# First four-head chunk inside the loop, and early half loads of the first values, in a cached decode-attention kernel

## The chip, the cores, the metric

One core of one Trainium2 chip. The metric is the device time of one execution in microseconds (us), median of several runs. All runs here are of the state called fast; with one core there is no other die to compare with.

## The reference, cut to what matters

Two independent decode attentions, one query token for each of four batch entries, bf16. Part A has 32 query heads on 8 key/value heads and looks at the last 2048 keys only. Part B has 32 heads of its own and looks at all 8192 keys. Part B's caches make up 537 MB of the 587 MB read.

```python
def _B_ref(x, k_cache, v_cache, wq, wo):        # A: the same with k, v repeated and Sk cut to W
    B, Sq, D = x.shape                          # 4, 1, 512
    H, Dh = 32, 128
    q = (x @ wq).reshape(B, Sq, H, Dh).transpose(0, 2, 1, 3)
    scores = jnp.einsum("bhqd,bhkd->bhqk", q, k_cache) * (Dh ** -0.5)   # Sk = 8192
    p = _softmax(scores, axis=-1)
    o = jnp.einsum("bhqk,bhkd->bhqd", p, v_cache)
    return o.transpose(0, 2, 1, 3).reshape(B, Sq, H * Dh) @ wo
```

## The kernel before

The work is cut into chunks: 8 of part A, then 32 of part B (four heads of one batch entry each). A chunk of part B has 8.39 MB of keys K and 8.39 MB of values V. TensorE transposes the keys (group `tr`), multiplies them with the query (`sc`), and after the softmax multiplies the values with the probabilities (`po`). In what follows the chunks of part B are called b0, b1, b2 and so on.

Pass c of part B does the keys of chunk c and the values of the chunk before. For b0 there is no chunk before, so it runs an "empty" value pass (`NONE`): 256 matmuls with probabilities of zero over whatever the value buffer holds. This keeps all passes alike.

```python
def whole_B(c):
    ch, p = chunks[c], prev(c)          # prev(first chunk) is NONE
    sch.mark()
    emit_qb(c)
    for g in range(ch["NG"]):           # 32 groups of 8 tiles
        emit_T(ch["s"] + g)             # transposes
        ...
    exp_B(c)                            # after out_B(p): values of the chunk before
```

All loads go through one transfer queue, in program order. Each has to wait until its buffer is free. Keys come in two halves (free when a half has been transposed), values as one transfer (free when the value pass has ended):

```python
def dma_B(kind, c):
    ...
    if kind == "k":
        pieces, fam = (NTB // 2,) * 2, "d_bk"
    else:
        pieces, fam = (LASTV, "d_lv") if c == NC - 1 else (NEXTV, "d_nv") if c == NC - 2 else ((NTB,), "d_bv")
    for i, n in enumerate(pieces):
        ...
        if kind == "v" and c == NCA:
            waits += [("pv", NONE)]     # V(b0) after the empty pass
        sch.add_dma("sp", ..., waits=waits, key=(kind, c, i))
    for u in range(4):
        held[at + u] = [("T", ...) if kind == "k" else ("pv", c)]

for c in range(NCA, NC):                # order: K(b0), K(b1), V(b0), K(b2), V(b1), ...
    dma_B("k", c)
    ...
    dma_B("v", c - 1)
```

A recording layer finds equal passes and emits them as one loop per engine. The first pass may join the loop if its waits, written with the loop's counter, are no weaker than its own. On TensorE and VectorE b0 did not qualify, so it stood as straight-line code ahead of the loop. For the head of TensorE's second loop the kernel asks for `head_slot` 0, taken here as the start of a block of 256 instruction slots (an estimate from the spacing of stalls, below), and a jump over padding leads into it.

Of the kernel before, what the change touches and what calls it, by code (L numbers as in the profile page):

```python
# [13 lines left out]
TG = 8  # L14
# [5 lines left out]
NSM = 2  # L20
SLAG = 2
NW = 64
NEXTV = (128, 64, 64)
LASTV = (128, 64, 32, 16, 8, 8)
QK = (0, 16)
# [2 lines left out]
TRM0, BC0, L0, Q0, XT0 = 0, 256, 288, 320, 448  # L28
# [19 lines left out]
class _Sched:  # L48
# [88 lines left out]
    def moved(self, ops, says, w, v, n, step, less=False):  # L137
        if says[w[0]:w[1]] != says[v[0]:v[1]]:
            return False
        new = dict(step)  # L140
        for k in range(w[1] - w[0]):
            x, y = self.needs(ops[w[0] + k][1]), self.needs(ops[v[0] + k][1])
            if ops[w[0] + k][3] is not None:
                x[k], y[k] = ops[w[0] + k][3], ops[v[0] + k][3]
            if less:
                if any(c not in x or y[c] > x[c] + n * new[c] for c in y) or any(x[c] + n * new[c] <= 0 for c in x):
                    return False
            elif set(x) != set(y) or any(y[c] - x[c] != n * new.setdefault(c, (y[c] - x[c]) // n) for c in x):
                return False
        step.update(new)  # L150
        return True
# [14 lines left out]
def bass_concat_heads__sliding_block_cached__mha_block_cached__decode_kernel(  # L166
# [29 lines left out]
    NC = len(chunks)  # L196
    NCA = Hkv
# [8 lines left out]
    NTA, NTB = chunks[0]["NT"], chunks[-1]["NT"]  # L206
    NONE = NC
    chunks.append(dict(chunks[NCA]))
    assert sum(LASTV) == sum(NEXTV) == NTB and NTA * 16 == 1024 and NTB * 4 == 1024

    sch = _Sched()
    with ExitStack() as es:
        block = es.enter_context(nc.Block())

        def sb(name, shape, dt):
            return es.enter_context(nc.sbuf_tensor(name, shape, dt))

        def ps(name, shape, dt):
            return es.enter_context(nc.psum_tensor(name, shape, dt))
# [3 lines left out]
        wos = sb("wos", [P, 4, DO], BF16)  # L223
        qb = sb("qb", [P, 2, NW], BF16)
        qq = sb("qq", [P, NW], BF16)
        wor = sb("wor", [P, NWO, 4 * DO], BF16)
        xs = sb("xs", [NB, 2, D], BF16)
        xT = sb("xT", [P, 2, KC * NB], BF16)
        qs = sb("qs", [P, 2 * NB * HQ + NW], BF16)
        identb = sb("identb", [P, P], BF16)  # L230
        identf = sb("identf", [P, P], F32)
        onesf = sb("onesf", [P, P], F32)
# [13 lines left out]
        pm = sb("pm", [P, HB + 1, NB, 4], F32)  # L246
        pbt = {0: sb("pba", [P, NPB, NTA * 16 + NW], BF16), 1: sb("pbb", [P, 1, NTB * 4 + NW], BF16)}
        oT = sb("oT", [P, NSM, 16], BF16)
# [8 lines left out]
        ms = ps("ms", [P, 512], F32)  # L257
# [2 lines left out]

        semnames = ["eng_pe", "eng_dve", "eng_act", "eng_pool", "eng_sp", "d_x0", "d_x1", "d_o0", "d_o1", "r_k", "r_v"]
        semnames += ["d_h%d" % i for i in range(NH)] + ["d_bk0", "d_bk1", "d_bv0"]
        semnames += [f + str(i) for f, x in (("d_lv", LASTV), ("d_nv", NEXTV)) for i in range(len(x))]
        semnames += ["d_wo%d" % i for i in range(NWO)] + ["d_wos"]
        sems = {n: es.enter_context(nc.semaphore(n)) for n in semnames}

# [12 lines left out]
        for u in range(4):  # L279
            sch.add("pool", lambda e, u=u: e.memset(rst[1][u * P // 4:(u + 1) * P // 4, u:u + 1], 1.0),  # L280
                    waits=["c_rs0"], key="c_rs" if u == 3 else None)
# [19 lines left out]
        held = [[] for _ in range(NH)]  # L301
# [10 lines left out]
        def flat(at, n):  # L312
            return kv[:, at:at + n, :].rearrange("p s x -> p (s x)")
# [21 lines left out]
        def dma_wos(hq):  # L335


            src = B_wo[4 * hq * P:4 * (hq + 1) * P, :].rearrange("(p r) n -> p (r n)", r=4)
            sch.add_dma("sp", lambda e: e.dma_start(wos[:, :, :].rearrange("p r n -> p (r n)"), src), "d_wos",
                        waits=[("fin", NCA + 4 * hq - 1)] if hq else [], key=("wos", hq))  # L340
# [6 lines left out]
            src = T[:, ch["g"], SkA - W:, :].rearrange("b (pp j) d -> pp b (j d)", pp=P // NB)  # L347
            sch.add_dma("sp", lambda e: e.dma_start(kv[:, at, :], src), "d_h%d" % at, waits=waits, key=(kind, c))

        def dma_B(kind, c):  # L350


            ch = chunks[c]
            T, at = (B_k, KB) if kind == "k" else (B_v, VB if c < NC - 1 else KB)
            src = T[ch["b"], 4 * ch["hq"]:4 * ch["hq"] + 4].rearrange("u (pp j) d -> (u pp) (j d)", pp=P // 4)
            dst = flat(at, 4)
            if kind == "k":
                pieces, fam = (NTB // 2,) * 2, "d_bk"
            else:
                pieces, fam = (LASTV, "d_lv") if c == NC - 1 else (NEXTV, "d_nv") if c == NC - 2 else ((NTB,), "d_bv")  # L360
            j0, unit = 0, NTB // 4
            for i, n in enumerate(pieces):
                waits = []
                for u in range(j0 // unit, (j0 + n - 1) // unit + 1):
                    waits += held[at + u]
                if kind == "v" and c == NCA:
                    waits += [("pv", NONE)]
                x = slice(j0 * P, (j0 + n) * P)
                sch.add_dma("sp", lambda e, x=x: e.dma_start(dst[:, x], src[:, x]), fam + str(i), waits=waits, key=(kind, c, i))
                if kind == "k" or c < NC - 1:  # L370
                    sch.relay("pool", sems, "r_" + kind, n // TG,
                              [(kind, c, i)] + ([("wos", ch["hq"])] if kind == "v" and i == 0 and ch["b"] == 0 else []))
                j0 += n
            for u in range(4):
                held[at + u] = [("T", ch["s"] + (u + 1) * unit // TG - 1) if kind == "k" else ("pv", c)]

        def landed(kind, c, g):

# [23 lines left out]
        for c in range(NCA, NC):  # L402
            dma_B("k", c)
            if c == NCA:
                dma_wos(0)
                sch.relay("pool", sems, "r_v", NTB // TG, [("wos", 0)])
                continue
            if c > NCA + 1 and (c - 1 - NCA) % NB == 0:
                dma_wos((c - 1 - NCA) // NB)
            dma_B("v", c - 1)  # L410
        dma_B("v", NC - 1)

        ms_read = []
        po_read = []
        rs_read = [[] for _ in range(NSM + 1)]

        def pe_mm(o, l, r, start=True, stop=True, transpose=False, waits=(), key=None):
            if transpose:
                sch.add("pe", lambda e: e.transpose(o, l, r), waits, key)  # L419
            else:  # L420
                sch.add("pe", lambda e: e.matmul(o, l, r, start=start, stop=stop), waits, key)  # L421
# [81 lines left out]
        def emit_S(s):  # L503
            c, g = groups[s]
            ch = chunks[c]
            for t in range(TG):
# [5 lines left out]

                n = min(NW, 512 - o0)
                q = qb[:, c % 2, 0:n] if ch["ab"] == 0 else qq[:, 0:n]
# [28 lines left out]
        def par(c):  # L543
            return c % 2 if c < NCA else 0
# [88 lines left out]
        def emit_pv(c, g):  # L633
            ch = chunks[c]
            UC = ch["UC"]
            base = 16 * (c % NSM) if ch["ab"] == 0 else 0
            for t in range(TG):
                j = g * TG + t
                n = NW
                waits = ([("exp", c)] if c != NONE else [("c_pb", 1)]) + po_read if j == 0 else []  # L640
                if j == 0:
                    po_read[:] = []
                if c >= NCA:
                    waits += landed("v", c, g) if t == 0 else []
                elif j == 0:
                    waits += [("v", c)]
                pe_mm(po[:, base:base + n], tile_of("v", c, j), pbt[ch["ab"]][:, par(c), j * UC:j * UC + n],
                      start=j == 0, stop=j == ch["NT"] - 1, waits=waits, key=("pv", c) if j == ch["NT"] - 1 else None)

        def norm_sum(c):  # L650
            if c < NCA:
                m, n, rs, ri = c % NSM, 16, rst[0][:, c % NSM, :], rinv[:, c % NSM, :]
            else:
                m, n, rs, ri = NSM, 4, rst[1][:, :], rinv[:, 0, 0:4]
            pe_mm(ms[:, L0:L0 + n], onesf[:, :], rs, waits=[("rs", c) if c != NONE else "c_rs", "c_onesf"] + ms_read, key=("L", c))
            sch.add("dve", lambda e: e.reciprocal(out=ri, in_=ms[:, L0:L0 + n]), waits=[("L", c)], key=("rinv", c))
            if c >= NCA:

                col = 16 * (c - NCA + 1 if c != NONE else 0)
                pv = pm[:, :, :, :].rearrange("p a b u -> p (a b u)")  # L660
                sch.add("dve", lambda e, x=0: e.tensor_tensor(
                    out=rz[:, :].rearrange("p (b u) -> p b u", b=NB), in0=bcast(ri, [[0, NB], [1, 4]]),
                    in1=pv[:, bass.ds(x + col, 16)].rearrange("p (b u) -> p b u", b=NB), op=ALU.mult),
                    waits=[("rinv", c), "c_pm"], key=("rz", c), at=col)
            ms_read[:] = [("rinv", c)]
            rs_read[m] = [("L", c)]
# [221 lines left out]
```

## Time and profile before

| | before |
|---|---|
| median of the runs on record with the result | 1393.03 us (1388.76 to 1394.37, 4 runs) |
| span of the profiled run | 1390.7 us |
| TensorE busy | 85% |
| read from memory | 587.21 MB, 422 GB/s over the span |

The prediction below shows the page, the windows and the transfer queue's timeline. One more view is needed to judge it afterwards: TensorE's timeline in b1's pass, the first time round the loop. Each line is start, length, engine, source line, operation, operands and count, and in brackets the idle time ahead of it with what ended it. "issue" means that nothing the profile records was waited for.

```profile
182.76 0.40 PE L419 MATMUL tr<-identb,kv 128*128 128x128 bf16 x4 [0.83 <-issue]
...
189.21 0.62 PE L419 MATMUL tr<-identb,kv 128*128 128x128 bf16 x8 [1.06 <-issue]
...
195.37 0.68 PE L421 MATMUL sc<-qq,kt 128*128 128x64 bf16 x20 [0.66 <-issue]
```

I read these, like the 7.51 us at the jump, as TensorE waiting for code, and call them code stalls. The DMA view, asked in steps of 0.1 us, has a packet of the instruction queue that starts at 180.5, 186.9 and 193.0 us, 2.3 to 2.4 us ahead of these three lines, as it has one at 165.9 us, 2.6 us ahead of the first line after the jump. The three lines stand 124 matmuls apart, and two such stalls inside a value pass stand 128 apart (shown below). A matmul counts as two instruction slots (the page has 27295 matmuls and as many weight loads), so a block of code is taken as 256 slots, an estimate from this spacing. The packets of the instruction queue are of 16 KB each (24 packets, 0.39 MB). In later passes of the loop the stalls do not occur: between 250 and 1340 us the view of waits lists none without a releaser, and the instruction queue has no such packet.

### The profile page before, as it was taken

What the parts mean: (1) busy time and instruction counts of PE and PEld (TensorE: products, weight loads), DVE (VectorE), ACT (ScalarE), POOL (GpSimd) and SP (SyncE); (2) the same over time, 40 slices, a digit from 0 to 9 for tenths busy, and PEclk for the clock granted to TensorE, in tenths of its full rate; (3) what the DMA queues carried; (4) which work ended last, traced back from release to release, by engine and by line L of the source; (5) the groups of instructions that cost most, each with busy time, mean ns of one, the idle gap of its engine ahead of it and who ended that gap; (6) DMA issues with size and microseconds to landing.
All of it is one profiled execution on the core that took longest, in us unless ns stands there. A gap on an engine that the chain in (4) does not pass through costs nothing.

```text
span 1390.7 us, 60414 instructions
## 1 busy us (share of the span) xinstructions
PE 1177.1 (85%) x27295; PEld 1124.9 (81%) x27295; DVE 682.5 (49%) x1532; ACT 482.1 (35%) x651; POOL 6.8 (0%) x27
## 2 busy tenths in 40 slices
PE   4898688888888878888888888888988878888887
PEld 4787688888887878888888778888878878888886
DVE  1776245555444444555444445555444444555442
ACT  1553223333333333333333332333333332333331
POOL 1000000000000000000000000000000000000000
PEclk9999899999999999999999999999999999999999
DMA  9999879999999999999999999999999999999998
GB/s 398 426 427 398 361 308 407 436 430 432 449 424 424 435 430 431 437 432 430 449 424 426 435 429 431 435 434 429 448 424 426 435 431 430 435 434 433 444 415 344
DMA packets 19797, 587.66 MB, mean 423 GB/s; under 512 B 2212, under 2 KB 2232, under 8 KB 4664
## 3 DMA queue, kind: packets, MB, share of 16 engines
q1 hardware_dynamic: 19736, 587.21, 98.4%
q8 instruction: 24, 0.39, 0.1%
q14 instruction: 5, 0.04, 0.0%
q10 hardware_dynamic: 32, 0.01, 0.0%
HBM read 587.21 MB, written 0.01 MB: 422 GB/s over the span
## 4 chain that ended last, share of the span: by engine, by line
DMA 62%; PE 33%; DVE 2%; issue 2%; SPq 0%; ACT 0%; DVEq 0%; POOLq 0%
DMA kv<-in_B_v_cache_dram 58%; PE po L421 22%; PE tr L419 6%; PE sc L421 3%; DMA kv<-in_B_k_cache_dram 2%; DMA kv<-in_B_wq_dram 2%; PE ms L421 1%; PE fin L421 1%; DVE sA L539 1%; DVE zB L698 0%; DVE rh L556 0%; DVE rm L551 0%; DVE kt L486 0%; DVE sA L537 0%; PE ms L419 0%
## 5 line engine op out<-in xcount | busy, mean ns | idle before, releaser
L419 PE MATMUL tr<-identb,kv 128*128 128x128 bf16 x8704 | 658.7, 220 | 13.3 <-issue 9.8
L486 DVE COPY kt<-tr 128x1024 bf16<-128x1024 bf16 x736 | 499.2, 691 | 212.9 <-PE tr L419 211.3
L419 PEld LDWEIGHTS tr<-identb,kv 128*128 128x128 bf16 x8704 | 509.4, 99 | 23.7 <-issue 19.0
L484 ACT ACTIVATE kt<-tr 128x1024 bf16<-128x1024 bf16 x352 | 359.3, 1023 | 388.1 <-PE tr L419 377.9
L421 PE MATMUL sc<-qq,kt 128*128 128x64 bf16 x8192 | 398.1, 191 | 11.1 <-DVE kt L486 9.5
L421 PE MATMUL po<-pbb,kv 128*128 128x64 bf16 x8448 | 312.0, 207 | 57.2 <-POOLq L70 55.0
L421 PEld LDWEIGHTS po<-pbb,kv 128*128 128x128 bf16 x8448 | 307.5, 108 | 60.3 <-POOLq L70 57.2
L421 PEld LDWEIGHTS sc<-qq,kt 128*128 128x128 bf16 x8192 | 328.7, 98 | 21.6 <-DVE kt L486 12.9
L596 ACT ACTIVATE pbb<-sc,negb 32x256 bf16<-32x256 f32 x128 | 105.4, 823 | 498.0 <-PE po L421 496.5
L678 DVE TENSOR_TENSOR oz<-po,rz 128x16 bf16<-128x16 f32 x33 | 5.8, 175 | 363.4 <-PE po L421 363.4
L556 DVE TENSOR_REDUCE rh<-sc 32x1 f32<-32x128 f32 x256 | 73.1, 286 | 17.2 <-PE sc L421 14.7
L419 PE MATMUL ms<-identf,rm 128*1 128x128 f32 (+1 forms) x40 | 11.4, 285 | 50.5 <-DVE rm L559 47.2
L419 PEld LDWEIGHTS ms<-identf,rm 128*1 128x1 f32 (+1 forms) x40 | 3.2, 80 | 54.4 <-DVE rm L559 50.1
L421 PE MATMUL fin<-wos,zB 128*4 128x256 bf16 x264 | 19.9, 272 | 26.6 <-DVE zB L698 26.1
L421 PEld LDWEIGHTS ms<-identf,gx 1*128 1x128 f32 (+1 forms) x80 | 13.5, 211 | 28.0 <-DVE gx L575 26.5
L421 PE MATMUL ms<-identf,gx 1*128 1x1 f32 (+1 forms) x80 | 17.0, 279 | 20.7 <-DVE gx L575 19.9
L421 PEld LDWEIGHTS fin<-wos,zB 128*4 128x4 bf16 x264 | 8.8, 82 | 31.1 <-DVE zB L698 29.7
L596 ACT ACTIVATION_READ_ACCUMULATOR pbb<-sc,negb 32x1 f32 x128 | 32.0, 250 | 0.0
L698 DVE CAST zB<-ms 32x16 bf16<-32x16 f32 x130 | 22.1, 170 | 13.0 <-PE ms L421 11.7
L421 PE MATMUL sc<-qb,kt 128*128 128x64 bf16 (+3 forms) x512 | 26.3, 197 | 0.4 <-DVE gx L575 0.4
L421 PEld LDWEIGHTS sc<-qb,kt 128*128 128x128 bf16 x512 | 22.0, 102 | 2.0 <-issue 1.1
L421 PE MATMUL po<-pba,kv 128*128 128x64 bf16 x512 | 20.1, 198 | 3.1 <-issue 1.7
(59 smaller groups left out, 205.0 us busy)
## 6 DMA issues: line engine op xcount, KB each, us to landing
kv<-in_B_k_cache_dram SPq DMA_DIRECT2D x64, 4096.0 KB, 25.6
kv<-in_A_k_cache_dram SPq DMA_DIRECT2D x8, 2048.0 KB, 13.1
kv<-in_A_v_cache_dram SPq DMA_DIRECT2D x8, 2048.0 KB, 14.6
kv<-in_B_v_cache_dram SPq DMA_DIRECT2D x2, 4096.0 KB, 23.4
kv<-in_B_v_cache_dram SPq DMA_DIRECT2D x3, 2048.0 KB, 26.3
kv<-in_A_wq_dram SPq DMA_DIRECT2D x1, 4096.0 KB, 12.3
kv<-in_B_wq_dram SPq DMA_DIRECT2D x1, 4096.0 KB, 27.2
wor<-in_A_wo_dram SPq DMA_DIRECT2D x8, 512.0 KB, 9.2
```

Source lines behind the costliest of these rows:

```text
L419: sch.add("pe", lambda e: e.transpose(o, l, r), waits, key)
L421: sch.add("pe", lambda e: e.matmul(o, l, r, start=start, stop=stop), waits, key)
L484: sch.add("act", lambda e: e.activation(dst, src, ACTF.Copy), waits=waits, key=("ev", s))
L486: sch.add("dve", lambda e: e.tensor_copy(dst, src), waits=waits, key=("ev", s))
L539: emit = lambda e, src=src, b=b: e.scalar_tensor_tensor(out=t, in0=src, scalar=mk[:, b:b + 1], in1=t, op0=ALU.mult, op1=ALU.add)
L556: sch.add("dve", lambda e, src=src, pp=pp: e.tensor_reduce(out=rh[pp, half:half + 1], in_=src, axis=AX.X, op=ALU.max), waits=[("S", ch["s" ...
L596: sch.add("act", lambda e, src=src, pp=pp, u=u: e.activation(probs_of(c)[pp, :, u], src, ACTF.Exp, bias=negb[pp, 0, 0:1], scale=scale, acc ...
L678: sch.add("dve", lambda e: e.tensor_tensor(out=o, in0=i0, in1=i1, op=ALU.mult), waits=waits, key=("oT", c))
L698: sch.add("dve", lambda e, src=src, dst=dst: e.tensor_copy(dst, src), waits=[("sm", c)] + free if h == 0 else [], key=("z", c) if h == (2 ...
```

## The change

Its intent is to keep the transfer queue filled where part A goes over into part B. V(b0) and V(b1) come in two halves. The first half of V(b0) is queued as soon as part A's value buffers are free, and each half of V(b1) when its half of the value pass before is done. The comparison of waits is changed and b0's waits get the form of the other passes', so that b0 joins the loop.

```diff
+FIRSTV = (128, 128)
@@ moved(): may the first pass join the loop?
-                if any(c not in x or y[c] > x[c] + n * new[c] for c in y) or any(x[c] + n * new[c] <= 0 for c in x):
+                if any(c not in x or y[c] > x[c] + n * new[c] for c in y) or any(type(c) is str and x[c] + n * new[c] <= 0 for c in x) \
+                        or any(type(c) is int and y.get(c) != x[c] + n * new[c] for c in x):
@@ dma_B
-                pieces, fam = ... (NEXTV, "d_nv") if c == NC - 2 else ((NTB,), "d_bv")
+                pieces, fam = ... (NEXTV, "d_nv") if c == NC - 2 else (FIRSTV, "d_fv") if c < NCA + 2 else ((NTB,), "d_bv")
-                if kind == "v" and c == NCA:
+                if kind == "v" and c == NCA and i == 1:
                     waits += [("pv", NONE)]
-                    sch.relay("pool", sems, "r_" + kind, n // TG, ...
+                    sch.relay("pool", sems, "r_" + kind, n // TG * (2 if kind == "v" and c == NCA else 1), ...
-                held[at + u] = [("T", ...) if kind == "k" else ("pv", c)]
+                    used[u] = [("T", ...) if kind == "k" else ("pv", c, "half") if u - at < 2 else ("pv", c)]
@@ order of the loads
-                sch.relay("pool", sems, "r_v", NTB // TG, [("wos", 0)])
+                dma_B("v", c, 0)
-            dma_B("v", c - 1)
+            dma_B("v", c - 1, 1 if c == NCA + 1 else None)
@@ emit_pv, norm_sum: the waits of b0's pass get the form of the other passes'
...
```

## The prediction

> **What bounds the kernel now.** I read the page first, its slices and its queues. In what follows b0, b1, b2 are the 32 four-head chunks in order (the kernel's chunks 8, 9, 10), K and V their keys and values, 8.39 MB each (two issues of 4096 KB).
>
> ```profile
> span 1390.7 us, 60414 instructions
> DMA  9999879999999999999999999999999999999998
> GB/s 398 426 427 398 361 308 407 436 430 432 449 424 424 435 430 431 437 432 430 449 424 426 435 429 431 435 434 429 448 424 426 435 431 430 435 434 433 444 415 344
> q8 instruction: 24, 0.39, 0.1%
> HBM read 587.21 MB, written 0.01 MB: 422 GB/s over the span
> ```
>
> The transfers are the bound: 587 MB at some 432 GB/s would take 1359 us. TensorE is busy 85% but not the limit. Only slices 4 to 6 (about 104 to 209 us), the passage from part A to part B, are much below the rest. So next the windows around that passage, with the long steady stretch as the yardstick. After the window and its length come each engine's busy time, then the granted clock, the DMA share and GB/s.
>
> ```profile
> 100.00:130.00 30.00, 25.34 (x457) 21.08 (x458) 17.79 (x53) 11.07 (x17) 0.00 (x0) 0.89 1.01 433
> 130.00:160.00 30.00, 25.49 (x614) 24.34 (x611) 13.47 (x31) 8.04 (x10) 0.00 (x0) 0.94 0.74 301
> 160.00:180.00 20.00, 12.08 (x212) 11.76 (x213) 6.87 (x14) 6.50 (x10) 0.00 (x0) 0.74 1.02 421
> 180.00:210.00 30.00, 24.83 (x577) 23.63 (x574) 12.19 (x27) 6.67 (x7) 0.00 (x0) 0.89 0.69 282
> 210.00:240.00 30.00, 26.75 (x633) 25.84 (x634) 19.10 (x41) 13.01 (x18) 0.00 (x0) 1.00 0.99 419
> ...
> 310.00:1350.00 1040.00, 894.48 (x20935) 861.84 (x20936) 509.85 (x1111) 360.30 (x481) 0.00 (x0) 0.93 1.00 432
> ```
>
> Two windows lose time: 30 x (1 - 0.74) = 7.8 us and 30 x (1 - 0.69) = 9.3 us, together **17 us in which the 16 DMA engines had nothing to do**. From 210 us on they never stop, so this loss is paid once and goes straight to the end. Third, the transfer queue's timeline (start, length, issues), to see why they had nothing:
>
> ```profile
> 100.12 0.91 SPq L369 DMA_DIRECT2D kv<-in_B_k_cache_dram  x2
> 101.07 0.43 SPq L339 DMA_DIRECT2D wos<-in_B_wo_dram  x1
> 133.11 12.46 SPq L369 DMA_DIRECT2D kv<-in_B_k_cache_dram  x2
> 159.10 0.33 SPq L369 DMA_DIRECT2D kv<-in_B_v_cache_dram  x1
> 181.50 13.45 SPq L369 DMA_DIRECT2D kv<-in_B_k_cache_dram  x2
> 209.46 0.33 SPq L369 DMA_DIRECT2D kv<-in_B_v_cache_dram  x1
> 222.19 11.20 SPq L369 DMA_DIRECT2D kv<-in_B_k_cache_dram  x2
> 244.52 0.33 SPq L369 DMA_DIRECT2D kv<-in_B_v_cache_dram  x1
> ```
>
> K(b0) and the output weights, issued at 100 to 101, are down at about 132. K(b1) waits until each half of K(b0) has been transposed (133.1, 145.2), V(b0) until the empty value pass inside b0 has ended (159.1), K(b2) for b1's transposes (181.5, 194.6), V(b1) for the value pass of b0 (209.5). Each time one thing is in flight, the queue drains, and TensorE must free a buffer before the next can start: six gaps that make up the 17 us.
>
> Last, TensorE's timeline where it goes from b0 (straight-line code) into the loop:
>
> ```profile
> 160.41 0.60 PE L421 MATMUL fin<-wos,zB 128*4 128x256 bf16 x8 [0.82 <-DVE zB L698]
> 168.52 2.74 PE L419 MATMUL tr<-identb,kv 128*128 128x128 bf16 x24 [7.51 <-issue]
> ```
>
> K(b1)'s first half had landed by 145 and no releaser is shown, yet TensorE stood 7.51 us. The DMA view has no packet of the instruction queue between 161 and 165.5 us and one between 165.5 and 168.5: it waited for code.
>
> [...] 24 packets of 0.39 MB are 16 KB each, and the stall is at the jump. [...] V(b0) was moving in 64 KB packets (17 packets, 1.11 MB between 161 and 165.5), and the fetch was late by about two of them. [...]
>
> **The change part by part.**
> (1) *V(b0) and V(b1) in halves.* V(b0)'s first half needs only part A's value buffers, free when part A's last value pass ends, at about 119.6. It is then queued behind K(b0), 12 us before the drain at 132. Its second half waits for the empty pass, as all of V(b0) did. V(b1)'s first half is released by the middle of b0's value pass, some 4.5 us before its end. No byte is added.
> (2) *b0 in the loop.* The same arithmetic; TensorE's program shrinks by 1566 of its 5909 instructions (counted in the order of instructions, a matmul as two). The jump moves from 161 to 121.4, the end of part A's last output product. There K(b0) is moving, in 32 KB rows. A 64 KB packet takes 65.5 KB / (421 / 16 GB/s) = 2.5 us, a 32 KB one 1.25 us. So I put the entry at 7.5 - 2 x 1.25 = **5 us (estimate)**, of which 0.6 is hidden, because K(b0)'s first half is there only at 122.1 anyway. After a stall the clock granted is low for a while (0.74 between 160 and 180; b1's first half took 13.0 us against 11.0 for b0's), so I allow up to 2 us more. The stall at 161 disappears: TensorE starts b1 at about 165 to 168 instead of 168.5.
> (3) *The queue played forward*, with 9.9 us per 4.19 MB half (419 to 424 GB/s) and 1.1 us from issue to first packet (209.46 issued, engines still empty in 209 to 210, moving in 210 to 211). b0 starts at 126.5; halves of a chunk take 11.0 to 12.4 us:
> V(b0)1 runs 132.7 to 142.6. K(b1)1 is issued at 137.5, without a gap, to 152.5. K(b1)2 is issued at 149.9, no gap, to 162.4. V(b0)2 is issued when the empty pass ends, 126.5 + 37 = 163.5, and moves at 164.6: gap 2.2, to 174.7. K(b2)1: b1 starts at 165.4, half done at 176.6, moves at 177.7: gap 3.0, to 188. K(b2)2 moves at 188.9: gap 0.9, to 199. V(b1)1 is issued at about 197: no gap, and from there the queue stays filled.
> Idle comes to about 6 us, 8 with the slow clock, against 17. **Saving: 17 - 6.5 = 10.5 us.** It persists: a steady loop pass needs 36.6 us of TensorE (from 283.0 to 321.3, the first transposes of two passes, less a wait of 1.7) against 38.8 us of transfer (16.78 MB at 432).
>
> **Rivals.**
> (a) *The entry costs nothing or all of the 7.5 us.* Without a stall b0 starts at 122.1 and the gaps shrink to some 2 us: saving 15. With 7.5 us plus a cold clock, V(b0)2 and K(b2) come 3 to 4 us later: saving 7.
> (b) *A new wait takes the place.* The empty pass multiplies zeros but now waits for V(b0)'s first half. By my queue that lands at 142.6 and is wanted at 149 or later, so it costs nothing; were it late, V(b0)2, and all behind it, would be late too and the saving would fall to 3 or 5.
> (c) *TensorE becomes the bound.* Speaking for it: 85% busy, slack of 2 us per pass. Against: in steady passes it waits for values each time (1.72 and 3.53 us ahead of the value passes at 310 and 350), and a saving moves both alike. It would eat a few us at most.
> (d) *Hidden anyway.* If the queue had slack later, nothing would change: 1393. The steady 432 GB/s speaks against it.
>
> **Range and chances.** The centre is 1393.8 - 10.5 = 1383.3 us. Rivals (a) and (b) span savings of about 5 to 15: 1378.5 to 1389. The whole idle time is 17 us, 1.2%, so a gain over 2% (27.9 us) is out of reach short of something unseen; a loss over 2% would need a new wait in every loop pass, and the loop's body is the same. Faster by over 2%: 0.01; within: 0.98; slower: 0.01.
>
> **What the next profile would show.** The queue's timeline: a half V at about 120, K(b1) at 137 and 150, the second half V near 163, K(b2) near 177, a half V near 197. The windows: 130 to 160 at a share of about 1 instead of 0.74, 160 to 210 with 6 to 8 us lost. TensorE: about 5 us of "issue" near 121 and none near 161. From 220 on, all as before but 10 us earlier. I would be wrong if the entry stall were much longer than 7.5 us, if the empty pass waited for its values, or if the steady passes ran at another rate.

## The result, and the profile after

The changed kernel took **1384.16 us** (median of 4 runs, 1383.07 to 1387.03) against 1393.03 us. The ratio is 0.9945, with a 95% interval of 0.9918 to 0.9971. Ratios here are the mean time of one kernel's fast runs over that of the other's of the same rounds, so not quite the ratio of the medians. In two later sets of rounds the same kernel had 0.9951 both times (labels e0_after_again and e10_after_beside below).

The transfer queue's timeline after:

```profile
119.81 0.33 SPq L374 DMA_DIRECT2D kv<-in_B_v_cache_dram  x1
134.21 12.60 SPq L374 DMA_DIRECT2D kv<-in_B_k_cache_dram  x2
165.20 0.33 SPq L374 DMA_DIRECT2D kv<-in_B_v_cache_dram  x1
180.24 11.21 SPq L374 DMA_DIRECT2D kv<-in_B_k_cache_dram  x2
200.39 4.06 SPq L374 DMA_DIRECT2D kv<-in_B_v_cache_dram  x2
```

V(b0)'s first half went out at 119.81, 39 us earlier than V(b0) before. But its second half went out at 165.20 (before: 159.10), and K(b2) at 180.24, only 1.3 us earlier than the 181.50 before. The windows show what this did:

```profile
130.00:160.00 30.00, 23.45 (x559) 22.77 (x557) 14.04 (x29) 7.43 (x8) 0.00 (x0) 0.94 1.00 425
160.00:180.00 20.00, 16.38 (x331) 15.46 (x328) 8.22 (x18) 7.83 (x13) 0.00 (x0) 0.83 0.57 233
180.00:210.00 30.00, 26.43 (x638) 25.30 (x636) 14.86 (x34) 10.20 (x16) 0.00 (x0) 0.94 0.93 376
...
310.00:1350.00 1040.00, 893.22 (x20946) 861.18 (x20943) 514.46 (x1120) 363.12 (x484) 0.00 (x0) 0.93 1.00 432
```

The hole at 130 to 160 us (share 0.74) is closed. A new one stands at 160 to 180 (1.02 before, 0.57 now). Only the third window is a clear gain, 0.69 before and 0.93 now. The steady stretch is as it was. TensorE's timeline at the entry and in b0's pass tells why (128 value matmuls stand between its last two stalls):

```profile
121.20 1.87 PE L428 MATMUL fin<-wor,zA 128*4 128x512 bf16 x4 [0.81 <-DVE zA L705]
123.00 2.12 PE L426 MATMUL tr<-identb,kv 128*128 128x128 bf16 x24
...
141.08 0.62 PE L426 MATMUL tr<-identb,kv 128*128 128x128 bf16 x8 [1.22 <-issue]
...
148.33 0.68 PE L428 MATMUL sc<-qq,kt 128*128 128x64 bf16 x20 [1.76 <-issue]
...
157.81 3.89 PE L428 MATMUL po<-pbb,kv 128*128 128x64 bf16 x128 [1.47 <-issue]
164.24 0.93 PE L428 MATMUL po<-pbb,kv 128*128 128x64 bf16 x26 [2.54 <-issue]
...
167.47 2.74 PE L426 MATMUL tr<-identb,kv 128*128 128x128 bf16 x24
```

There is no stall at the jump (123.00). In its place there are four code stalls in b0's pass, 1.22 + 1.76 + 1.47 + 2.54 = 7.0 us. Each time it goes on 2.5 to 2.6 us after a packet of the instruction queue has started (at 138.6, 145.7, 155.2 and 161.6 us). In ten profiles of this document I looked up 39 such stalls: all ended 2.2 to 2.8 us after the start of such a packet. The pass from the first transpose to the end of the values took 165.2 - 123.0 = 42 us, against 37 before. b1 therefore starts at 167.47, not much before the 168.52 of the kernel before.

The idle time of the transfer engines at the passage can be read from windows: the sum of length x (1 - share) over 130 to 170, 170 to 210 and 210 to 250 us. It is good to 1 or 2 us: a share can come out above 1 (1.03 in one window of e1, e4, e7 and e10), and then counts as up to 1.2 us less idle time. It is used in the table of the experiments.

### The profile page after: what moved, and what is told of

The parts are those of the page before. It is cut to its first block, busy times and chain, and to the rows that moved or that the text cites. A ratio compares the mean times of both kernels' runs of the same rounds, so it can differ in the third digit from the quotient of the medians.

```text
span 1385.2 us, 60499 instructions
## 1 busy us (share of the span) xinstructions
PE 1172.5 (85%) x27294; PEld 1122.1 (81%) x27295; DVE 682.5 (49%) x1532; ACT 482.3 (35%) x651; POOL 6.8 (0%) x27
## 4 chain that ended last, share of the span: by engine, by line
DMA 62%; PE 34%; DVE 2%; issue 2%; SPq 0%; ACT 0%; DVEq 0%; POOLq 0%
DMA kv<-in_B_v_cache_dram 58%; PE po L428 22%; PE tr L426 7%; PE sc L428 3%; DMA kv<-in_A_k_cache_dram 2%; DMA kv<-in_B_wq_dram 2%; PE fin L428 1%; PE ms L428 1%; DVE zB L705 0%; DVE sA L546 0%; DVE rh L563 0%; PE ms L426 0%; DVE gm L578 0%; SPq L341 0%; DVE oz L685 0%
## 5 line engine op out<-in xcount | busy, mean ns | idle before, releaser
L705 DVE CAST zB<-ms 32x16 bf16<-32x16 f32 x130 | 22.1, 170 | 13.0 <-PE ms L428 11.7
```

What stands on the lines that cost most here:

```text
L705: sch.add("dve", lambda e, src=src, dst=dst: e.tensor_copy(dst, src), waits=[("sm", c)] + free if h == 0 else [], key=("z", c) if h == (2 ...
```

## The experiments

Theory T, formed on this result: *the passage is set by TensorE's progress through b0 and the first half of b1, because K(b2) can't be asked for before. Where V(b0) stands in the queue hardly matters.* Rival P, on which most of the predicted saving rests: *the gain is that V(b0)'s early half fills the drain at 132 us.* A second question is what makes the code stalls: where the jump stands within a block of 256 slots (the layout theory), or the size of the data packets.

| kernel | median us | ratio to before | span of profile | idle 130 to 250 | span less idle |
|---|---|---|---|---|---|
| before | 1393.0 | 1 | 1390.7 | 16.0 | 1374.7 |
| changed | 1384.2 | 0.9945 | 1385.2 | 11.2 | 1374.0 |
| changed, again (e0) | 1385.3 | 0.9951 | 1386.2 | 10.8 | 1375.4 |
| changed, again (e10) | 1385.1 | 0.9951 | 1380.1 | 6.8 | 1373.3 |
| e1 loop only | 1384.4 | 0.9949 | 1380.9 | 8.8 | 1372.1 |
| e2 halves only | 1388.9 | 0.9981 | 1388.6 | 15.2 | 1373.4 |
| e3 changed, shifted | 1386.8 | 0.9963 | 1385.2 | 9.2 | 1376.0 |
| e4 before, shifted | 1388.4 | 0.9985 | 1384.8 | 10.0 | 1374.8 |
| e7 small rows | 1382.5 | 0.9942 | 1381.0 | 5.2 | 1375.8 |
| e6 no empty pass | 1381.7 | 0.9936 | 1379.2 | 6.0 | 1373.2 |
| e8 = e6 and e7 | 1382.0 | 0.9936 | 1380.3 | 3.2 | 1377.1 |
| e9 = e6, four chunks in halves | 1379.4 | 0.9908 | 1379.0 | 4.0 | 1375.0 |

The last column is the same within 5 us in twelve profiles, where the spans differ by 11.7 us: most of what a version loses or gains is the idle time of the transfer engines at the passage. The profiled runs differ from the medians by up to 4 us. The medians come from four sets of rounds, in which the kernel before itself had 1391.4 to 1393.0, so the ratios decide, and a profile shows how.

### e0_after_again and e10_after_beside: the changed kernel unchanged

> The changed kernel unchanged, for a second profile and more times beside the other variants. 7 to 10 us below the kernel before (1383 to 1386 us). The profiled run of it so far was the slowest of its four and had four code stalls of TensorE inside the first loop pass (1.2 + 1.8 + 1.5 + 2.5 = 7.0 us). If these stalls vary from run to run and set the time, a profile of a run at 1383 to 1384 has 3 to 5 us of them instead of 7; if they are fixed by the layout they are again about 7 us.

Measured: 1385.33 us (6 runs), ratio 0.9951 (0.9924 to 0.9978). The profiled run, 1388.05 us, again had four code stalls in b0's pass, 1.2 + 1.8 + 1.7 + 2.0 = 6.7 us, and K(b2) went out at 180.06.

> The changed kernel once more, as the yardstick on the same chip and rounds: 1383 to 1386 us, 0.994 to 0.996 of the kernel before.

Measured: 1385.10 us, ratio 0.9951 (0.9933 to 0.9968). Its profiled run was its fastest, 1381.81 us. The stalls in b0's pass were again 6.3 us (0.28 + 1.61 + 2.86 + 0.68 + 0.89), so the guess that they alone make the difference was wrong. This time b1's first half took less: 12.7 us from V(b0)'s second issue to K(b2)'s, against 15.0 and 15.2 in the two slower runs (164.76 to 177.47 in the queue's timeline). In the run shown above, one of the slower two, the last stall (2.54 us) was followed by a granted clock of 0.83 in 160 to 180 us, and b1's first 24 transposes took 2.74 us, not the 1.51 us that the same group took in a later pass.

### e1_loop_only

b0 in the loop, but V(b0) and V(b1) whole, as before:

```diff
-                ... else (FIRSTV, "d_fv") if c < NCA + 2 else ((NTB,), "d_bv")
+                ... else ((NTB,), "d_bv")
-                if kind == "v" and c == NCA and i == 1:
+                if kind == "v" and c == NCA:
-                dma_B("v", c, 0)
+                sch.relay("pool", sems, "r_v", NTB // TG, [("wos", 0)])
...
```

> The first four-head chunk in the loop, but V(b0) and V(b1) whole and released as before. Theory T (TensorE's progress through b0 and the first half of b1 sets the passage; early values hardly matter): b0 starts at 123 as in the changed kernel, K(b2) is issued at about 180, V(b1) at about 204, total 2 to 3 us above the changed kernel (1386 to 1388). Rival P (the gain is that V(b0)'s early half fills the drain at 132 us): the drain is back and most of the gain is gone, 1390 to 1393.

Measured: 1384.35 us, ratio 0.9949 (0.9922 to 0.9975), in the same rounds in which the changed kernel had 0.9951. **Without its halves the change gains the same.** Rival P falls, and theory T's 2 to 3 us for the halves were too much as well. The queue and TensorE show why:

```profile
133.24 13.44 SPq L374 DMA_DIRECT2D kv<-in_B_k_cache_dram  x2
161.22 0.33 SPq L374 DMA_DIRECT2D kv<-in_B_v_cache_dram  x1
173.93 11.21 SPq L374 DMA_DIRECT2D kv<-in_B_k_cache_dram  x2
197.76 0.33 SPq L374 DMA_DIRECT2D kv<-in_B_v_cache_dram  x1
```

```profile
140.94 0.62 PE L426 MATMUL tr<-identb,kv 128*128 128x128 bf16 x8 [1.88 <-issue]
...
147.10 0.68 PE L428 MATMUL sc<-qq,kt 128*128 128x64 bf16 x20 [0.66 <-issue]
...
156.29 4.89 PE L428 MATMUL po<-pbb,kv 128*128 128x64 bf16 x154 [1.15 <-issue]
```

The drain at 132 is back, but the code stalls are 3.7 us, not 7.0, and the empty pass ends at 161.2. K(b2) goes out at 173.9, and from there on nothing is lost. The last line is one group of 154 value matmuls: the boundary after its first 128, where the changed kernel stood 2.54 us, cost nothing here, with V(b0) not yet issued. In the DMA view the code came later where the transfer engines were busier. Counted from the first matmul of the block before, the code packet started after 3.8 us in the changed kernel (157.81 to 161.6; the transfer engines' share was 0.99 in 158 to 159 us), after 2.3 us in e10 (share 0.61 in 159 to 160) and after 1.5 us here (156.29 to 157.8; share 0.15 in 157 to 158). These are three single profiles, so it is a correlation. The 2.5 us or so from the packet to the next matmul were paid in the changed kernel even while the transfer engines stood idle (share 0.00 from 162 to 165 us).

### e2_halves_only

The halves, with b0 kept out of the loop on TensorE and VectorE. TensorE's program then has exactly as many instructions as before:

```diff
-            if n > 1 and a > 0 and self.moved(...
+            if n > 1 and a > 0 and not (engname in ("pe", "dve") and a == 6) and self.moved(...
```

> Values in halves as in the changed kernel, but the first four-head chunk stays straight-line code on TensorE and VectorE, so TensorE's program has the same length as before (jump at the same place, 13 slots into a block). Theory T: the stall at the jump near 161 us is still there, 4 to 7.5 us, K(b2) is issued near 178 to 181, the half release of V(b1) still helps: 1385 to 1388. Rival P: all the gain comes from the halves, the same as the changed kernel, 1383 to 1385, with 130 to 160 us at a DMA share of 1.0.

Measured: 1388.86 us, ratio 0.9981 (0.9953 to 1.001). Its six times lie above all six of e1 in the same rounds (1386.92 to 1392.16, against 1382.73 to 1384.85). Most of the gain is gone, although the windows show 130 to 170 us well filled (0.94; the kernel before had 0.82, from the same windows):

```profile
130.00:170.00 40.00, 27.34 (x655) 25.90 (x652) 15.27 (x36) 11.02 (x16) 0.00 (x0) 0.90 0.94 396
170.00:210.00 40.00, 34.72 (x773) 33.92 (x773) 18.53 (x37) 10.41 (x11) 0.00 (x0) 0.88 0.70 281
```

The jump's stall is still there, 5.90 us, and K(b2) goes out at 183.83, so the engines lose after 170 us what they won before (15.2 us idle in all).

```profile
170.85 2.74 PE L426 MATMUL tr<-identb,kv 128*128 128x128 bf16 x24 [5.90 <-issue]
```

### e3_after_shift and e4_before_shift: the place of the jump

Counting slots from two observed stalls, with blocks of 256 as estimated above, the kernel before jumps 13 slots into a 256-slot block, and the changed kernel 237 slots into one. Repeating tiny transposes while TensorE waits for its first weights swaps these places: two more rounds of eight (32 slots) for the changed kernel, fourteen (224 slots) for the kernel before. Nothing else is changed.

```diff
-                    pe_mm(o, xv[:, r, :], identb[0:NB, 0:NB], transpose=True, ...
+                    for again in range(SHIFT):      # 3 in the changed kernel, 15 in the kernel before
+                        pe_mm(o, xv[:, r, :], identb[0:NB, 0:NB], transpose=True, ...
```

> The changed kernel with 16 more tiny transposes (32 instruction slots) while TensorE waits for its first weights, which moves the jump into the loop from 237 slots into a 256-slot block to 13 slots into the next one, where the kernel before has it. Layout theory [...]: a stall of 4 to 7 us appears at about 122 us, b0 starts at 126 to 129, total 2 to 5 us above the changed kernel. Rival (the stall before came from the 64 KB packets alone, or a jump costs nothing here): no stall at 122, the same time as the changed kernel.

Measured: 1386.75 us, ratio 0.9963 (0.9936 to 0.999), 1.4 us above the changed kernel of the same rounds by the medians. A stall appears at the jump, 2.24 us and not 4 to 7, with 3.3 us more in the pass:

```profile
126.80 2.74 PE L427 MATMUL tr<-identb,kv 128*128 128x128 bf16 x24 [2.24 <-issue]
```

The times of the two kernels lie too close to be called different (the intervals overlap), and in the profiled run K(b0) was issued 1.5 us later from the start (101.64 us against 100.14). The stall itself followed the layout: none with the jump at 237 slots, 2.24 us at 13.

> The kernel before with 224 more instruction slots of tiny transposes while TensorE waits for its first weights: its jump into the loop moves from 13 slots into a 256-slot block to 237 slots into it, where the changed kernel has it. Nothing else is changed: b0 stays outside the loop, values whole. Layout theory: [...] the stall of 7.5 us near 161 shrinks to 0 to 3 us, K(b2) is issued at 175 to 178 instead of 181.5, and 3 to 6 us of the gain come by padding alone: 1387 to 1390. Rival [...]: stall and time as before, 1392 to 1394.

Measured: 1388.38 us, ratio 0.9985 (0.997 to 1.0). The stall at the jump, 7.51 us, shrank to 0.18 us, and K(b2) went out at 173.41 instead of 181.50. But b1's pass then had four stalls, 1.08 + 2.10 + 1.61 + 1.76 = 6.6 us, where the kernel before had 2.8:

```profile
161.41 1.51 PE L420 MATMUL tr<-identb,kv 128*128 128x128 bf16 x24 [0.18 <-issue]
```

So in these four profiles the stall went with where the jump stands: 7.51 and 2.24 us at 13 slots, 0.18 us and none at 237. The place isn't all of it: in e8 and e9 below, with the jump at 241 slots, TensorE stood 0.99 us (ahead of 197.24) and 2.03 us (ahead of 196.13) there. Padding alone brings 2 to 3 us of the 8, barely clear of noise (the interval reaches 1.0), since much of it comes back as stalls at block boundaries, in a pass that runs through the loop's code for the first time while V(b0) moves.

### e7_small_rows

The changed kernel with K and V of b0 and b1 issued as four transfers instead of one (8 KB rows for 32 KB):

```diff
+                cuts = ROWS if c < NCA + 2 and n == 128 else 1      # ROWS = 4
+                for q in range(cuts):
+                    x = slice((j0 + q * n // cuts) * P, (j0 + (q + 1) * n // cuts) * P)
+                    sch.add_dma("sp", ..., waits=waits if q == 0 else [], key=(kind, c, i) if q == cuts - 1 else None)
```

> The changed kernel with K and V of b0 and b1 issued as four transfers in place of each one, so that rows are 8 KB instead of 32 KB; same bytes, same order. Theory T ([...] TensorE's progress sets the passage): the stalls in the first pass fall from 7 us to 0 to 3 us, K(b2) is issued at 175 to 177 instead of 180, total 2 to 4 us below the changed kernel, 1381 to 1383. Rival (the stalls do not depend on packet size): four stalls of together 6 to 7 us again and the time of the changed kernel, or a little more from shorter rows.

Measured: 1382.53 us, ratio 0.9942 (0.9929 to 0.9955). The stalls in b0's pass were 0.68 + 0.94 + 0.98 + 2.54 = 5.1 us, so they fell by 2 us and not by 4 to 7. The last one, in the value pass, didn't move at all. From the start of one block's code (155.86) to that of the next (162.29) it took 6.4 us, as in the changed kernel (157.81 to 164.24), while the value pass needs 3.9 us for a block. The code packet itself started 3.8 us after the block before it in both (159.7 us here). Packet size is at most a part of the wait. Whether the kernel became faster than the changed one isn't settled: the intervals overlap, and it was not run in the same rounds.

### e6_no_empty and e8_no_empty_small

The test that theory T asks for: let TensorE be done earlier. b0 does no value pass at all, and V(b0)'s second half waits for its buffer only. b0 and b1 are straight-line code, padded as in e4 so that the jump stands 241 slots into a block.

```diff
-                if kind == "v" and c == NCA and i == 1:
-                    waits += [("pv", NONE)]
-                if g == 8:
+                if g == 8 and p != NONE:
                     norm_sum(p)
-            out_B(p)
+            if p != NONE:
+                out_B(p)
...
```

> The changed kernel without the empty value pass: b0 does no value pass at all (its and b1's code are straight-line, padded so that the jump stands 241 slots into a block), V(b0)'s second half waits for nothing but its buffer. Theory T (TensorE sets the passage: 8 to 13 us of empty pass before K(b2) can be asked for): b1 starts near 153 instead of 167, K(b2) is issued at 165 to 170 while V(b0) is still moving, idle time of the transfer queue between 130 and 250 falls from 11 us to 0 to 3, total 7 to 10 us below the changed kernel, 1374 to 1378. Rival (a little idle is left however early TensorE is[...]): 1380 to 1384.

Measured: 1381.73 us, ratio 0.9936 (0.9923 to 0.9949), the result still correct. K(b2) went out at 165.86, as expected, and up to 210 us nothing is lost. But 7 to 10 us below the changed kernel were expected, and about 3 came by the medians and 1 to 2 by the ratios. The intervals overlap and the two were not run in the same rounds, so a gain over the changed kernel isn't shown:

```profile
130.00:160.00 30.00, 24.01 (x509) 23.26 (x506) 17.77 (x35) 13.52 (x18) 0.00 (x0) 0.94 1.00 427
160.00:200.00 40.00, 34.67 (x767) 33.55 (x764) 18.95 (x42) 12.63 (x18) 0.00 (x0) 0.87 1.00 423
200.00:250.00 50.00, 41.98 (x955) 40.32 (x952) 23.99 (x51) 17.43 (x22) 0.00 (x0) 0.93 0.87 364
```

The hole has moved to b2: it is now the first pass of the loop, with stalls of 0.77, 1.61 and 2.03 us, and V(b2), one whole transfer, waits for the end of its value pass at 237.00.

> Both of the last two together: no empty pass, and 8 KB rows for K and V of b0 and b1. Theory T: if the version without the empty pass keeps the queue filled, the smaller rows add nothing (same time within 1.5 us, 1374 to 1378); if it still shows idle time from code stalls, this one removes it and is 1 to 4 us faster than it.

Measured: 1382.03 us, ratio 0.9936 (0.9923 to 0.9948), no different from e6. The small rows add nothing there.

### e9_halves_four

The hole of e6 stands ahead of V(b2), so its remedy is the one that the change used for V(b1): halves, for four chunks.

```diff
-                ... (FIRSTV, "d_fv") if c < NCA + 2 else ...
+                ... (FIRSTV, "d_fv") if c < NCA + 4 else ...
```

> The version without the empty pass, with the values of the first four chunks of part B in halves instead of two. In the version before this one the queue was idle for 5.6 us at 232 to 238 us, because V(b2) whole waits for the end of b1's value pass. If a half of V(b2) can start at the middle of that pass, the gap falls to 0 to 2 us and the span to its floor (spans less the idle time between 130 and 250 us were 1372 to 1377 us in the ten profiles so far): span 1374 to 1377, time 1376 to 1379, 2 to 5 us below the version without the empty pass. Rival (the lost time moves on to a later chunk, because TensorE is late by then): the gap comes back after 250 us and the time stays at 1381 to 1383.

Measured: **1379.41 us** (1377.7 to 1381.17), ratio 0.9908 (0.989 to 0.9926). The changed kernel had 1385.10 and 0.9951 (0.9933 to 0.9968) in the same rounds, so this version beats both kernels and is correct.

```profile
170.00:210.00 40.00, 33.41 (x751) 32.00 (x747) 18.39 (x41) 12.49 (x17) 0.00 (x0) 0.91 1.00 420
210.00:250.00 40.00, 32.61 (x700) 31.24 (x698) 16.72 (x39) 11.54 (x17) 0.00 (x0) 0.87 0.89 363
```

4 us of idle time are left in the profiled run, all of it after 210 us.

## Why the prediction was right or wrong

The time was right: 1383.3 predicted, 1384.16 measured, inside the range. Of its steps, some held and others cancelled out, so that it came so close was partly luck. (A slip without effect: V(b0)'s second half, moving from 164.6 for 9.9 us, ends at 174.5 and not at 174.7; the idle time is still about 6 us.)

- **The bound held.** The transfers bound the kernel, the loss at the passage is paid once, and the steady 432 GB/s, at a DMA share of 1.00 from 310 to 1350 us, are unchanged. The nearly constant last column of the table shows it for twelve profiles.
- **"V(b0)'s first half ... queued ... 12 us before the drain" held as a fact and failed as a gain.** It went out at 119.81 and the drain was gone. e1 without it is as fast. The prediction had K(b2) wait for b1's transposes, rightly. What its playing forward lacked is that TensorE came later where the queue was fuller: in the profiles, b0's values ended at 165.2 us and K(b2) went out at 180.2 with the early half (164.8 and 177.5 in e10), and at 161.2 and 173.9 without it. Where TensorE didn't arrive earlier, filling the queue only moved the idle time (e2: share 0.94 in 130 to 170 us, then 0.70).
- **"The entry at 5 us (estimate)" failed.** There was no stall (b0 starts at 123.00, and at 122.10 in the kernel before). The estimate took the stall as a matter of packet size: two packets of 64 KB (17 of them took 2.4 us each between 161 and 165.5 us) shrinking to two of 32 KB. That code waits behind data packets in this way was my assumption, and no run shows it: what the trace shows is that the code packet started at 165.9 us, 4.9 us after TensorE's last work. In e3 and e4 the stall went with where in its block the jump stands: 7.51 and 2.24 us at 13 slots, 0.18 us and none at 237. At 13 slots the size still varies (5.90 us in e2), at 241 slots e8 and e9 have 0.99 and 2.03 us, and what sets it isn't separated. Rival (a) had foreseen an entry without a stall, but with a saving of 15 us. That didn't come, because of the next point.
- **b0's pass at 37 us failed.** It took 42 us, because the first time round the loop costs code stalls (7.0 us) that the prediction had left at the 1.3 us of the straight-line b0. Zero at the entry and 5 us more in the pass put b1's start at 167.5, where 165.4 was predicted: two errors that nearly cancel, by luck.
- **Idle time: 6 to 8 us predicted, 11.2 in the profiled run** and 6.8 in the fastest profiled one. The saving by the medians was 8.9 us, and 7 to 8 us by the ratios, against 10.5 predicted.
- **Rival (b) didn't occur:** the empty pass began at 151.69, right behind the product ahead of it, with no wait for V(b0). **Rival (c) didn't either:** the stretch from 310 to 1350 us is unchanged.
- **Where the gain came from:** b0 in the loop. It takes away the 7.5 us at 161, and b1's pass has no code stall (2.8 us in the kernel before; in the changed one the instruction queue has no packet from 161.7 to 206.7 us), so that K(b2)'s second half and V(b1) go out 3.5 and 9 us earlier (191.4 for about 194.9, 200.4 for 209.5). How much of it is the jump and how much the boundaries isn't separated: e4 took the jump's stall away and got others. e2 kept b0 out of the loop on TensorE and VectorE together. The stalls are TensorE's, but VectorE's share wasn't run apart.

## What to carry to other kernels

Where a queue runs dry, ask first what the next transfer but one is waiting for: if it is an engine, filling the gap with something else may gain nothing (here 0.9951 with the early half loads and 0.9949 without, in the same rounds). The first pass through the loop had its own stalls here (6.3 to 7.0 us in the changed kernel, none between 250 and 1340 us). They moved with the layout of the code (7.51 and 0.18 us at the jump of the kernel before) and, it seems, with the load on the transfer engines (3.8, 2.3 and 1.5 us to the code packet at shares of 0.99, 0.61 and 0.15). Leaving out a piece of work (e6, 0.9936) brought more than placing the jump well (e4, 0.9985, in the same rounds). When a prediction is right, undo its parts one at a time all the same: here the part that was taken for the main cause added nothing that the runs can tell.

## What the profiles show of the code stalls

- At block boundaries, the first time round: up to 3.06 us for one (e2, in the empty pass), and 6.3 to 7.0 us in b0's pass of 42 us in three profiles of the changed kernel. Between 250 and 1340 us none of these three has one.
- At the jump into the loop: 7.51 and 0.18 us in the kernel before with two paddings, 0 and 2.24 us in the changed one. With the jump at 241 slots, 0.99 us in e8 and 2.03 us in e9.
- In the value pass, from one block's first matmul to the next one's: 6.4 us twice (changed kernel and e7), 5.9 (e0) and 4.8 us (e10), where the pass itself needs 3.9 us for the 128 matmuls. From the start of a block's packet to its first instruction: 2.2 to 2.8 us in 39 stalls.
- With 8 KB rows instead of 32 KB (e7), the stalls of one pass fell from 7.0 to 5.1 us only, and the longest (2.54 us) not at all.
